# Transposing 18 of 32 blocks by DMA, as two 16-bit planes, in a transformer block on one Trainium2 core

## The chip, the core and the metric

The kernel runs on one core of a Trainium2 chip: TensorE (PE in the profile; PEld is its weight load), VectorE (DVE), ScalarE (ACT), GpSimd (POOL) and the queue engine SyncE (SP), each with its own in-order stream of instructions, and 16 DMA engines. The metric is the device time of one execution in microseconds, the median of three runs. The profile is one execution recorded by the hardware profiler.

## The reference

One pre-norm transformer block on 2048 rows of 512 floats, in float32.

```python
x = A_x                                          # (1, 2048, 512)
h = x + attention(layernorm(x), wqkv) @ wo       # 32 heads of 16; row s sees rows s, s-2, ..., s-14
n = layernorm(h)
r = relu(n @ w1 + b1)                            # 512 -> 1792
out = h + (r * r) @ w2 + b2                      # 1792 -> 512
```

Attention is local and dilated: each row has 8 keys (window 8, dilation 2), masked where the position is negative, softmax over the 8.

## The kernel before

**Numbers in two parts.** Every float32 matrix is split into a rounded part and the rest (`hi` on ACT, L141, and `lo` on DVE or POOL, L144); a product is three products of parts, so `mm3` (L224) is 12 matmuls of 128x128 by 128x512. A contraction needs the contracted dimension on the partitions, so three things are transposed on PE: the normalised input (`x_T`), attention's result (`o_T`) and the normalised residual (`h_T`). `transposes` (L199) is four 128x128 matmuls with the identity into one PSUM bank; `hi_T` and `lo_T` then read that bank and write the two parts. The second and fourth tile of the last group are transposed by the same four matmuls at L638.

**Tiles and stages.** The rows are 16 tiles `t` of 128, in 4 groups `u` of 4 tiles; t = 4u + i. Stage one computes q, k, v of tiles 0 to 3; stage two (`first_phase`, called for t0 = 4, 6, ..., 14) those of the other tiles, two a phase, in 12 half slots `m` a phase; a running number `k` = 12 (t0/2) - 72 + m gives the half slot relative to the phase of t0 = 12. Then come three loops over `u` = 0, 1, 2 with 17 slots `p` each: slot p holds a first-layer product `mlp1` (L224, from p = 0 to 13) and a second-layer product `mlp2` (L808, from p = 3 to 16) of group u. In the same slots group u + 1 goes through attention's tail: `load_h`, `o_T`, `wo_product` (L224, `wo<-`), the residual sum `h_add` (L577, DVE), `h_norm` (L194, ACT), `add_b2` (L587, POOL), a spill to memory, and `h_T`, whose parts are the input of the next loop. The last group (u = 3) has a stage of its own with seven products of halves (L731).

**Attention** runs on DVE and POOL beside all this: for each chunk `s` of two tiles (8 chunks) and each group of 4 heads (8), DVE multiplies (L335), sums (L369) and weighs (L346) blocks of 128x1024, POOL adds up the weighed blocks (L403, the last of three sums writes `o`), ACT copies q to PSUM (L264) and takes the exponentials (L392), and SP loads windows of k and v (L243) and q (L256) from memory, two steps ahead. A chunk is done after 8 sums into its `o`.

**The order** is written out by the program itself (a manual schedule): each engine executes in the order in which the Python code emits. `at(d, f, ...)` puts a call at the end of the slot d slots on, `after` behind it; `end_slot` runs the due calls, then `pump`. `pump` (L409 on) emits attention's steps as long as its own running estimate of DVE's time, `now["dve"]`, is below that of PE's, `now["pe"]`; an attention step counts as its cost times a factor from `SLOW`: the first for the stages before the loops, the second for loop u = 0, the third for the loops after. `transposes` adds 0.44 to PE's estimate. `pump(until=s)` emits attention until chunk s is done, whatever the estimates say; `o_T` calls it. `OT`, `WO`, `HT` are the half slots k of `o_T`, `wo_product`, `h_T` for tiles 0 to 3; `OP`, `WP`, `HP` the slots p for the four tiles of each later group (`HL` replaces `HP` in loop u = 2).

**Buffers.** Tiles named with `row(...)` share 15 buffers of 128x512 float32. In the loops the products and the transposes take turns on two PSUM banks (`mm0`, `mm1`).

Of the kernel before, what the change touches and what calls it, by code (L numbers as in the profile page):

```python
# [7 lines left out]

F32 = mybir.dt.float32
F32R = mybir.dt.float32r  # L10
AF = mybir.ActivationFunctionType
ALU = mybir.AluOpType
X = mybir.AxisListType.X
# [2 lines left out]
P = 128  # L16
KB = D // P
FB = F // P
R = 4
RI = 2  # L20
# [7 lines left out]
NEG = -4.0e9  # L28
ROWS = 15
LAG = 3  # L30
SLOW = 1.01, 1.12, 1.08
DELAY = 3
WJ = 2
XT = (9, 11), (7, 8)
OT = 4, 5, 10, 12
WO = 7, 9, 13, 15
HT = 20, 20, 21, 23
W2 = (18,)
LH = 3, 4, 10, 11
OP = 6, 7, 12, 13  # L40
WP = 8, 9, 13, 14
HP = 15, 15, 16, 16
UP = 14, 14, 15, 15
HL = (14, 0), (14, 1), (15, 0), (15, 1)
# [8 lines left out]
def block_kernel(ctx, tc, x, wqkv, wo, w1, b1, w2, b2, out):  # L53
    nc = tc.nc
# [3 lines left out]
    att = ctx.enter_context(tc.tile_pool(name="att", bufs=2))  # L58
# [27 lines left out]

    big_h = wpool.tile([P, 3 * KB, D], F32R, name="big_h")
    big_l = wpool.tile([P, 3 * KB, D], F32R, name="big_l")
    wq_h, wq_l = [t.rearrange("p (k c) n -> p k (c n)", k=KB) for t in (big_h, big_l)]
    wo_h = wpool.tile([P, KB, D], F32R, name="wo_h")  # L90
    wo_l = wpool.tile([P, KB, D], F32R, name="wo_l")
    w1_h = wpool.tile([P, KB, F], F32R, name="w1_h")
    w1_l = wpool.tile([P, KB, F], F32R, name="w1_l")
    w2_h, w2_l = {}, {}

    def row(name, shape=(P, D), dt=F32):
        return work.tile(list(shape), dt, name=name, tag="row", bufs=ROWS)
# [8 lines left out]
    def at(delta, fn, *a):  # L106
        due.setdefault(now["slot"] + delta, []).append((fn, a))
# [61 lines left out]
    def act_stats(key, src):  # L169
# [4 lines left out]
        scrap = row("scrap")  # L174
        nc.scalar.activation(scrap, src, AF.Identity, accum_out=nm[:, 0:1])
        nc.scalar.activation(nm[:, 1:2], nm[:, 0:1], AF.Identity, scale=-1.0 / D)
# [30 lines left out]
    def hi_T(tr, h_dst):  # L207
        for d, src in parts(tr, h_dst):
            hi(d, src)

    def lo_T(tr, h_dst, l_dst):
        for (d, src), h in zip(parts(tr, l_dst), h_dst):
            lo(nc.vector, d, src, h)
            dve(0.16 + 0.53 / len(h_dst))
# [16 lines left out]
    o_t = {}  # L231
# [177 lines left out]
    def pump(until=None):  # L409

        while (done[until] < G) if until is not None else (now["dve"] < now["pe"]):
            todo = sums[:]
            sums.clear()
            t = next(stream, "end")
            for a in todo:
                add_up(*a)
            if t == "end":
                now["dve"] = 1e9
                return
            if t is None:  # L420
                now["dve"] = max(now["dve"], now["pe"])
                return
            dve(t * SLOW[min(now['sub'] + 1, 2)])

# [126 lines left out]
    hs, hn = {}, {}  # L551
    oT = {}
# [9 lines left out]
    def o_T(t):  # L562
        s, j = divmod(t, RI)
        pump(until=s)
        tr = transposes(o_t[s][:, j, :])
        if t % R == RI:

            ohl = att.tile([P, 2, KB, P], F32R, name="ohl", tag="o", bufs=3)
            oT[t] = ohl[:, 0], ohl[:, 1]
        else:  # L570
            oT[t] = row("oh", (P, KB, P), F32R), row("ol", (P, KB, P), F32R)
        at(0, hi_T, tr, [oT[t][0]])
        at(0, lo_T, tr, [oT[t][0]], [oT[t][1]])

    def h_add(t, ps):
        h = hs[t]
        nc.vector.tensor_tensor(out=h, in0=ps, in1=h, op=ALU.add)  # L577
        dve(0.7)
        norm_stats(t, h)
# [16 lines left out]
    def wo_product(t, slots):  # L596
# [4 lines left out]
        for n, (fn, a) in zip(slots, ((h_add, (t, ps)), (h_norm, (t,)), (add_b2, (t,)),  # L601
# [5 lines left out]
    hh, hl = [[big_l[:, n:n + 2].rearrange("p k (i c) -> p k i c", i=R) for n in ns]  # L607
              for ns in ((0, 3), (6, 9))]

    def h_T(t):  # L610
        if t // R == R - 1:
            return last_h_T(t)
        tr = transposes(hn.pop(t), "mm")
        i = t % R
        hs_, ls_ = [a[:, :, i] for a in hh], [a[:, :, i] for a in hl]
        if len(turn["mm"].tags) > 2:
            at(0, hi_T, tr, hs_)
        else:
            due.setdefault(now["slot"], []).insert(0, (hi_T, (tr, hs_)))
        at(0, lo_T, tr, hs_, ls_)  # L620
# [7 lines left out]
    last_tr, banks = {}, {}  # L628
# [260 lines left out]
    for n in range(16):  # L889
        gp, t = divmod(n, 4)  # L890
# [27 lines left out]
    def first_phase(t0):  # L918
        def chores(m):
            if t0 + 3 < 16:  # L920
                if m in (0, 2):
                    at(0, x_stats, t0 + 2 + m // 2)

                early = t0 == 12
                if m + early in (6, 7):
                    at(0, x_norm, t0 - 4 + m + early)
                if m in XT[early]:
                    x_T(t0 + 2 + XT[early].index(m))
            if t0 + 5 < 16 and m in (6, 9):
                at(0, load_x, t0 + 2 + m // 3)  # L930
            if jobs and m % 3 == 0:
                at(0, weight_job)
            k = t0 // 2 * 12 - 72 + m
            if k == 19:
                dve(HOLD)
            for t in range(R):
                if k == OT[t]:
                    at(0, load_h, t)
                    o_T(t)
                if k == WO[t]:  # L940
                    wo_product(t, (1, 3, 4, 6))
                    now["pe"] += 2.73
                if k == HT[t]:
                    h_T(t)
            if k in W2:
                at(0, load_w2, W2.index(k))

        def half(m):
            end_slot(1.37)
            chores(m)  # L950

        for n in range(6):
            chores(2 * n)
            qkv_of(t0 + n % 2, n // 2, lambda: half(2 * n + 1))
            end_slot(1.37)
# [41 lines left out]
    for u in range(R - 1):  # L997
        now["sub"] = u
        first, end = u == 0, False
        fs = list(range(FB)) if first else [*sorted(place), 12, 13]  # L1000
        fs += [f for f in range(12) if f not in fs and (u < 2 or f not in ENDS)]
        fs += ENDS if u == 2 else []
        need = [] if first else [f for f in fs if f < 12 and f not in place]
        acc = [psum.tile([P, D], F32, name="acc", tag=tag) for tag in ("acc0", "acc1", "tr0", "tr1")]
        js = range(R)


        todo, halves = {}, {}
        for i in js:
            t = R * (u + 1) + i  # L1010
            if not end:
                a = i // 2 if u == 2 else 0
                for p, *what in ((LH[i] - a, at, 0, load_h, t), (OP[i] - a, o_T, t),
                                 (WP[i] - a, wo_product, t, (0, 1, 2 + 3 * a, 3 + 3 * a))):
                    todo.setdefault(p, []).append(what)
                p, h = (HP[i], i % 2) if u < 2 else HL[i]
                (todo, halves)[h].setdefault(p, []).append((h_T, t))
            todo.setdefault(UP[i], []).append((at, 0, unspill, R * u + i))
        if u == 2:
            for p, *what in ((12, at, 0, t_load, 0), (12, at, 0, t_load, 1), (13, after, 0, t_sums, 0),  # L1020
                             (13, after, 0, t_sums, 1), (13, at, 1, t_split, 0),
                             (14, after, 0, t_split, 1)):
                todo.setdefault(p, []).append(what)

        def half(p):
            run(due)
            for fn, *a in halves[p]:
                fn(*a)

        for p in range(FB + LAG):  # L1030
            more = 0.0
            if p == FB:
                run(due)
                dve(HOLD)
            if u < 2 and p == FB - 2:
                dve(HOLD)
            for fn, *a in sorted(todo.get(p, []), key=lambda x: x[0] is wo_product):
                fn(*a)
                more += 2.73 if fn is wo_product else 0.0
            if p < FB:  # L1040
                mlp1(u, fs[p])
                more += 2.73
                if first:
                    at(0, split_w2, p)
                    if p + 1 < FB:
                        load_w2(p + 1)
            q = p - LAG
            if q >= 0:
                f = fs[q]
                mlp2(u, f, acc, js, q == 0, q == FB - 1,  # L1050
                     (lambda: half(p)) if p in halves else None)
                more += 2.74
                if f < 12 and (need or first and p < FB - LAG):
                    free.append(place.pop(f))
                    if need:
                        at(1, fetch, need.pop(0))
            end_slot(more)
        for i in js:
            at(u // 2, finish, R * u + i, acc[i])
# [48 lines left out]
    h = hs[S // P - 1]  # L1108
# [34 lines left out]
```

## Time and profile before

| what | value |
|---|---|
| median of 3 runs | 514.47 us (514.29 to 515.16) |
| the profiled execution | span 513.0 us from the first to the last instruction; the page has no other time of it |
| PE, PEld busy | 506.4, 429.3 us |
| DVE, POOL, ACT busy | 376.7, 350.0, 256.2 us |
| matmuls that transpose | x 64, `o` 64, normalised residual 56 + 8 |
| moved by DMA | 97.37 MB, mean 190 GB/s |

A row of a grouped view reads: line, engine, operation, what is written and read, shapes, count, then busy time in us and the mean of one in ns, then the engine's idle time just before these instructions and what ended it. A row of the time line has the start in us from the span's beginning, the duration, and merged neighbours as x4. A row of the waits reads: who waited for whom, us in total, times, longest. Matmuls overlap in the records, so the step from one to the next is their price, not their duration.

### The profile page before, as it was taken

What the parts mean: (1) busy time and instruction counts of PE and PEld (TensorE: products, weight loads), DVE (VectorE), ACT (ScalarE), POOL (GpSimd) and SP (SyncE); (2) the same over time, 40 slices, a digit from 0 to 9 for tenths busy, and PEclk for the clock granted to TensorE, in tenths of its full rate; (3) what the DMA queues carried; (4) which work ended last, traced back from release to release, by engine and by line L of the source; (5) the groups of instructions that cost most, each with busy time, mean ns of one, the idle gap of its engine ahead of it and who ended that gap; (6) DMA issues with size and microseconds to landing.
All of it is one profiled execution on the core that took longest, in us unless ns stands there. A gap on an engine that the chain in (4) does not pass through costs nothing.

```text
span 513.0 us, 7625 instructions
## 1 busy us (share of the span) xinstructions
PE 506.4 (99%) x2508; PEld 429.3 (84%) x2508; DVE 376.7 (73%) x524; ACT 256.2 (50%) x498; POOL 350.0 (68%) x430
## 2 busy tenths in 40 slices
PE   7999999999999999999999999999999999999997
PEld 6999788888888888888888888888888888989996
DVE  5489799988998798976889799778984035742333
ACT  4634687767424763463364334336432525666542
POOL 4714888894885895896778759676889544685520
PEclk9999999999999999999999999999999999999999
DMA  9677989889677895685487537557632352454112
GB/s 265 193 221 188 271 283 315 275 274 278 196 234 201 291 299 173 175 232 180 129 266 229 163 94 231 174 160 257 219 94 65 106 159 84 142 145 145 63 41 82
DMA packets 88239, 97.37 MB, mean 190 GB/s; under 512 B 8328, under 2 KB 56712, under 8 KB 88200
## 3 DMA queue, kind: packets, MB, share of 16 engines
q1 hardware_dynamic: 87256, 96.37, 61.4%
q10 hardware_dynamic: 944, 0.52, 0.3%
q8 instruction: 19, 0.31, 0.3%
q14 instruction: 20, 0.16, 0.1%
HBM read 72.65 MB, written 24.25 MB: 189 GB/s over the span
## 4 chain that ended last, share of the span: by engine, by line
PE 92%; POOL 3%; DMA 2%; DVE 1%; issue 1%; ACT 1%; SPq 0%; POOLq 0%; ACTq 0%
PE mm L224 45%; PE acc L808 29%; PE wo L224 9%; PE mm L731 6%; PE tr L199 4%; DMA wraw<-in_A_wqkv_dram 1%; DMA qkv_d<-y 1%; POOL pr L403 1%; POOL h L587 1%; POOL tl L144 0%; PE half L831 0%; SPq L432 0%; POOL wo_l L144 0%; DVE pr L346 0%; DVE ex L369 0%
## 5 line engine op out<-in xcount | busy, mean ns | idle before, releaser
L403 POOL TENSOR_TENSOR pr<-pr 128x512 f32<-128x512 f32 (+1 forms) x128 | 132.1, 1032 | 51.2 <-DVE pr L346 45.7
L224 PE MATMUL mm<-big_l,w_h 128*128 128x512 f32 x336 | 89.5, 392 | 0.0
L346 DVE TENSOR_TENSOR pr<-ex,v 128x1024 f32<-128x1024 f32 x64 | 78.0, 1221 | 11.6 <-POOL o L403 7.6
L335 DVE TENSOR_TENSOR pr<-qp,k 128x1024 f32<-128x1024 f32 x64 | 76.8, 1201 | 5.7 <-ACT qp L264 5.7
L369 DVE TENSOR_REDUCE ex<-pr 128x64 f32<-128x1024 f32 x64 | 78.4, 1225 | 1.8
L224 PEld LDWEIGHTS mm<-big_l,w_h 128*128 128x128 f32 x336 | 62.3, 188 | 12.8 <-DVE ol L144 0.2
L144 POOL TENSOR_TENSOR rl<-r,rh 128x512 fp32r<-128x512 f32 x42 | 55.4, 1318 | 22.5 <-ACT rh L141 22.4
L224 PE MATMUL mm<-big_h,xl 128*128 128x512 f32 (+1 forms) x208 | 55.9, 379 | 0.2 <-DVE xl L144 0.2
L224 PE MATMUL mm<-big_h,xh 128*128 128x512 f32 (+1 forms) x208 | 53.5, 378 | 0.7 <-ACT xh L141 0.7
L784 ACT ACTIVATE r<-mm,b_sb 128x512 f32<-128x512 f32 x42 | 28.8, 686 | 47.9 <-PE mm L224 46.1
L224 PE MATMUL mm<-big_l,xh 128*128 128x512 f32 (+1 forms) x208 | 52.7, 375 | 0.0
L808 PE MATMUL acc<-big_l,rh 128*128 128x512 f32 x190 | 52.7, 391 | 0.0
L808 PE MATMUL acc<-big_h,rh 128*128 128x512 f32 x190 | 52.3, 392 | 0.0
L808 PE MATMUL acc<-big_h,rl 128*128 128x512 f32 x190 | 51.8, 390 | 0.0
L493 ACT COPY y<-mm 128x512 f32<-128x512 f32 (+1 forms) x52 | 28.6, 552 | 40.0 <-PE mm L224 30.1
L224 PE MATMUL mm<-big_l,w_l 128*128 128x512 f32 x168 | 45.0, 390 | 0.0
L224 PEld LDWEIGHTS mm<-big_h,xh 128*128 128x128 f32 x208 | 37.6, 188 | 7.0 <-ACT xh L141 1.7
L224 PEld LDWEIGHTS mm<-big_l,xh 128*128 128x128 f32 x208 | 38.2, 188 | 6.0
L224 PEld LDWEIGHTS mm<-big_h,xl 128*128 128x128 f32 x208 | 37.2, 188 | 5.7 <-DVE xl L144 0.6
L808 PEld LDWEIGHTS acc<-big_h,rl 128*128 128x128 f32 x190 | 35.7, 188 | 7.5
L808 PEld LDWEIGHTS acc<-big_l,rh 128*128 128x128 f32 x190 | 35.4, 188 | 7.3
L808 PEld LDWEIGHTS acc<-big_h,rh 128*128 128x128 f32 x190 | 34.8, 188 | 6.5
(148 smaller groups left out, 879.8 us busy)
## 6 DMA issues: line engine op xcount, KB each, us to landing
k<-qkv_d SPq DMA_DIRECT2D x48, 288.0 KB, 2.8
v<-qkv_d SPq DMA_DIRECT2D x48, 288.0 KB, 4.0
qkv_d<-y SPq DMA_DIRECT2D x18, 512.0 KB, 4.3
big_l<-w2l_d SPq DMA_DIRECT2D x24, 256.0 KB, 3.1
xt<-in_A_x_dram SPq DMA_DIRECT2D x16, 256.0 KB, 4.3
q<-qkv_d SPq DMA_DIRECT2D x32, 128.0 KB, 3.0
h<-in_A_x_dram SPq DMA_DIRECT2D x16, 256.0 KB, 4.1
h_d<-h SPq DMA_DIRECT2D x16, 256.0 KB, 4.1
```

What stands on the lines that cost most here:

```text
L144: eng.tensor_tensor(out=dst, in0=src, in1=h, op=ALU.subtract)
L199: nc.tensor.transpose(tr[:, k, :], src[:, k * P:(k + 1) * P], ident)
L224: nc.tensor.matmul(ps, l(k), r(k), start=(n == 0), stop=(n == 3 * KB - 1))
L335: nc.vector.tensor_tensor(out=pr.rearrange("p i w h d -> p i w (h d)"), in0=qps["now"][:, j % 2].unsqueeze(2).to_broadcast([P, RI, W, GC]) ...
L346: nc.vector.tensor_tensor(out=p2, in1=vwin, op=ALU.mult, in0=e1[:, :, :, j * GH:(j + 1) * GH].unsqueeze(4).to_broadcast([P, RI, W, GH, DH]))
L369: nc.vector.tensor_reduce(out=lf[:, :, :, j * GH:(j + 1) * GH], in_=pr, axis=X, op=ALU.add)
L403: nc.gpsimd.tensor_tensor(out=dst, in0=p2[:, :, :w], in1=p2[:, :, w:2 * w], op=ALU.add)
L493: nc.scalar.copy(y[:, :, t % RI * GC:(t % RI + 1) * GC], ps[:, :j * GC].rearrange("p (j c) -> p j c", j=j))
L587: nc.gpsimd.tensor_tensor(out=h, in0=h, in1=b2_sb, op=ALU.add)
L731: nc.tensor.matmul(ps, sta[y][:, k], mov[x][:, k], start=(first and q == 0), stop=(last and q == len(terms) - 1), skip_group_check=True)
L784: nc.scalar.activation(r, ps, AF.Relu, bias=b1_sb[:, f:f + 1])
L808: nc.tensor.matmul(acc[j], l[:, j * P:(j + 1) * P], w[f], start=(first and n < len(js)), stop=(last and n >= len(terms) - len(js)))
```

## The change

For tiles in `OV` (10 of attention's 16) and `HV` (8 of the 16 normalised residuals) the transposition leaves PE. A float32 block of 128x512 is copied by ACT into two planes of 16-bit halves (split), SP issues one transposing DMA of the 128x1024 16-bit elements back into the source's buffer, eight blocks of 128x128, and ACT puts the halves together again (join); `hi_T` and `lo_T` then read this SBUF tile instead of a PSUM bank. Split, DMA and join stand in three slots: for tiles 0 to 3 by `OK` and `HK`, in the loops from `OP` on (o0, o0 + 1, o0 + 2), and from `WP` + 2 on for the residual. In the loops the `wo` products of each group's first two tiles move one slot later (`WP`). The second and third pacing factor are lowered.

```diff
-SLOW = 1.01, 1.12, 1.08
+OV = (0, 1, 2, 3, 4, 5, 8, 9, 12, 13)
+HV = (0, 1, 4, 5, 8, 9, 12, 13)
+SLOW = 1.01, 1.10, 1.06
+OK = (-6, -2, 4), (-5, -1, 5), (3, 6, 10), (4, 7, 12)
+HK = (12, 15, 18), (14, 16, 19)
-WP = 8, 9, 13, 14
+WP = 9, 10, 13, 14
+    def turn_split(key, src):
+        planes[key] = src, row("pl")
+        nc.scalar.copy(two_planes(planes[key][1]), halves_of(src))
+
+    def turn_dma(key):
+        src, pl = planes[key]
+        nc.sync.dma_start_transpose(
+            src.bitcast(U16).rearrange("p (n c) -> p n c", c=P), pl.bitcast(U16))
+
+    def turn_join(key):
+        src, pl = planes[key]
+        nc.scalar.copy(halves_of(pl).rearrange("p two n -> p n two"),
+                       two_planes(src).rearrange("p two n -> p n two"))
+        planes[key] = pl.rearrange("p (k c) -> p k c", k=KB)
+
+    def o_split(t):
+        s, j = divmod(t, RI)
+        pump(until=s)
+        turn_split(("o", t), o_t[s][:, j, :])
+
+    def o_join(t):
+        turn_join(("o", t))
+        tr = planes.pop(("o", t))
...
+        hi_T(tr, [oT[t][0]])
+        lo_T(tr, [oT[t][0]], [oT[t][1]])
+
+    def h_split(t):
+        turn_split(("h", t), hn.pop(t))
+
+    def h_parts(t):
+        i = t % R
+        tr = planes.pop(("h", t))
+        if t // R == R - 1:
+            last_tr[i] = tr
+            split_last(i, tr)
+            return
...
+        hi_T(tr, hs_)
+        lo_T(tr, hs_, ls_)
                 if k == OT[t]:
                     at(0, load_h, t)
-                    o_T(t)
+                    if t not in OV:
+                        o_T(t)
+                if t in OV and k in OK[t]:
+                    at(0, (o_split, lambda t: turn_dma(("o", t)), o_join)[OK[t].index(k)], t)
+                if t in HV and k in HK[t]:
+                    at(0, (h_split, lambda t: turn_dma(("h", t)),
+                           lambda t: turn_join(("h", t)))[HK[t].index(k)], t)
...
-                    h_T(t)
+                    (at(0, h_parts, t) if t in HV else h_T(t))
...
-                for p, *what in ((LH[i] - a, at, 0, load_h, t), (OP[i] - a, o_T, t),
+                o0 = OP[i] - a
+                if t in OV:
+                    turned = [(o0, at, 0, o_split, t), (o0 + 1, at, 0, turn_dma, ("o", t)),
+                              (o0 + 2, at, 0, o_join, t)]
+                else:
+                    turned = [(o0, o_T, t)]
+                if t in HV:
+                    h0 = WP[i] - a + 2
+                    turned += [(h0, at, 0, h_split, t), (h0 + 1, at, 0, turn_dma, ("h", t)),
+                               (h0 + 2, at, 0, turn_join, ("h", t))]
...
-                (todo, halves)[h].setdefault(p, []).append((h_T, t))
+                if t in HV:
+                    todo.setdefault(p, []).append((at, 0, h_parts, t))
+                else:
+                    (todo, halves)[h].setdefault(p, []).append((h_T, t))
```

More of the change, by code (lines that the diff above doesn't have):

```diff
@@ L10 @@
 F32R = mybir.dt.float32r
+U16 = mybir.dt.uint16
 AF = mybir.ActivationFunctionType
@@ L573, in o_T, with halves_of, two_planes @@
         at(0, lo_T, tr, [oT[t][0]], [oT[t][1]])
+    planes = {}
+    def halves_of(a):
+        return a.bitcast(U16).rearrange("p (n two) -> p two n", two=2)
+    def two_planes(a):
+        return a.bitcast(U16).rearrange("p (two n) -> p two n", two=2)
+    def turn_split(key, src):
[17 more added lines that the diff above has]
+        tr = planes.pop(("o", t))
+        if t % R == RI:
+            ohl = att.tile([P, 2, KB, P], F32R, name="ohl", tag="o", bufs=3)
+            oT[t] = ohl[:, 0], ohl[:, 1]
+        else:
+            oT[t] = row("oh", (P, KB, P), F32R), row("ol", (P, KB, P), F32R)
+        hi_T(tr, [oT[t][0]])
[9 more added lines that the diff above has]
+            return
+        hs_, ls_ = [a[:, :, i] for a in hh], [a[:, :, i] for a in hl]
+        hi_T(tr, hs_)
+        lo_T(tr, hs_, ls_)
     def h_add(t, ps):
@@ L1012, in block_kernel @@
                 a = i // 2 if u == 2 else 0
-                for p, *what in ((LH[i] - a, at, 0, load_h, t), (OP[i] - a, o_T, t),
+                o0 = OP[i] - a
[8 more added lines that the diff above has]
+                               (h0 + 2, at, 0, turn_join, ("h", t))]
+                for p, *what in ((LH[i] - a, at, 0, load_h, t), *turned,
                                  (WP[i] - a, wo_product, t, (0, 1, 2 + 3 * a, 3 + 3 * a))):
@@ L1016, in block_kernel @@
                 p, h = (HP[i], i % 2) if u < 2 else HL[i]
-                (todo, halves)[h].setdefault(p, []).append((h_T, t))
+                if t in HV:
+                    todo.setdefault(p, []).append((at, 0, h_parts, t))
+                else:
+                    (todo, halves)[h].setdefault(p, []).append((h_T, t))
             todo.setdefault(UP[i], []).append((at, 0, unspill, R * u + i))
```

## The prediction, as it was made before the result

> **What bounds the kernel now.** First the busy times and the chain that ended last, both on the page of the profile.
>
> ```profile
> span 513.0 us, 7625 instructions
> PE 506.4 (99%) x2508; PEld 429.3 (84%) x2508; DVE 376.7 (73%) x524; ACT 256.2 (50%) x498; POOL 350.0 (68%) x430
> ...
> PEclk9999999999999999999999999999999999999999
> ...
> PE 92%; POOL 3%; DMA 2%; DVE 1%; issue 1%; ACT 1%; SPq 0%; POOLq 0%; ACTq 0%
> ```
>
> TensorE (PE) is busy 506.4 of 513.0 us at a granted clock in the top digit in all 40 slices, and 92% of the last chain is its own work. So PE time that goes away is time saved, as long as nothing makes PE wait instead. Next I read the windows, one row a stage, for the engines that could (us, then busy time of PE, PEld, DVE, ACT, POOL, then clock, DMA share, GB/s).
>
> ```profile
> 120.00:162.00 42.00, 42.00 (x206) 34.91 (x205) 37.34 (x53) 18.93 (x40) 27.08 (x38) 1.00 0.76 230
> 162.00:210.00 48.00, 48.00 (x217) 39.70 (x216) 41.45 (x50) 27.17 (x48) 37.01 (x39) 1.00 0.75 237
> 210.00:254.00 44.00, 43.98 (x206) 35.94 (x205) 35.24 (x49) 19.32 (x38) 36.64 (x42) 1.00 0.66 194
> 254.00:300.00 46.00, 46.00 (x208) 38.10 (x207) 40.59 (x49) 20.63 (x36) 30.40 (x33) 1.00 0.62 190
> 300.00:345.00 45.00, 45.00 (x212) 37.26 (x211) 37.06 (x50) 17.70 (x34) 36.15 (x46) 1.00 0.59 181
> 345.00:390.00 45.00, 45.00 (x204) 37.24 (x203) 39.13 (x47) 20.02 (x34) 35.38 (x39) 1.00 0.57 181
> ```
>
> While attention runs, PE never idles. VectorE (DVE) is busy 37.34 + 41.45 + 35.24 + 40.59 + 37.06 + 39.13 = 230.8 of 270 us, so 39 us are free; ScalarE (ACT) is under 60% and the DMA engines under 76%. DVE is the engine nearest to PE. The view of waits says why part of its idle time is there, and how little PE waits for what the change touches (total, times, longest):
>
> ```profile
> DVE h L577 <- PE wo L224: 16.9, 11, 6.5
> ...
> PEld tr L199 <- ACT hn L194: 0.4, 1, 0.4
> ...
> PEld mm L224 <- DVE ol L144: 0.2, 1, 0.2
> ```
>
> DVE stands 16.9 us waiting for PE's `wo` product: it runs ahead of PE, and those waits shrink by themselves if PE comes earlier.
>
> **The change, part by part. Removed from PE:** 18 blocks of four transposes. The price of a block is read from the time line as the distance between the same matmuls with and without one between them.
>
> ```profile
> 218.19 1.07 PE L808 MATMUL acc<-big_h,rh 128*128 128x512 f32 x4
> ...
> 223.63 1.07 PE L808 MATMUL acc<-big_h,rh 128*128 128x512 f32 x4
> ...
> 226.35 0.60 PE L199 MATMUL tr<-ident,o 128*128 128x128 f32 x4
> ...
> 229.54 1.07 PE L808 MATMUL acc<-big_h,rh 128*128 128x512 f32 x4
> ```
>
> Without a block 223.63 - 218.19 = 5.44 us pass, with one 229.54 - 223.63 = 5.91, so a block holds PE 0.47 us. 18 x 0.47 = 8.46 us go. This is the only term on the path, and the greatest gain there can be.
>
> **Added to ACT:** two copies a block (split and join), 36 in all, each of 1024 16-bit elements. Rows of the grouped view, busy us, then mean ns:
>
> ```profile
> L141 ACT CAST rh<-r 128x512 fp32r<-128x512 f32 x56 | 34.8, 622 | 2.2
> ...
> L144 DVE TENSOR_TENSOR rl<-r,rh 128x512 fp32r<-128x512 f32 x14 | 11.8, 842 | 22.5 <-ACT rh L141 21.2 <-POOL traw L701 1.3
> ...
> L144 DVE TENSOR_TENSOR ol<-tr,oh 128x512 fp32r<-128x512 f32 x12 | 8.3, 690 | 10.3 <-ACT oh L141 10.1 <-POOL w_l L144 0.2
> ...
> L141 ACT CAST th<-traw 128x1024 fp32r<-128x1024 f32 x7 | 7.3, 1050 | 4.9 <-POOL traw L702 4.9
> ...
> L141 ACT CAST oh<-tr 128x512 fp32r<-128x512 f32 x12 | 7.0, 586 | 8.5 <-PE tr L199 8.5
> ```
>
> No row has 16-bit elements. The ends are 0.62 us (a 512-element row, if two halves go as one word) and 2.1 (twice the 1024-element row, if 16-bit strides cost double); I take 1.05, the row with as many elements. That is 37.8 us: 12.6 around the first phases' window of 120 to 162, where ACT has 42 - 18.9 = 23 free, and 25.2 over the three loops, where about half of it is free. PE hides it; at 2.1 us the first phases would lack 2 us. The casts and subtractions now read SBUF instead of PSUM: 622 against 586 ns on ACT, up to 842 against 690 on DVE, together at most 18 x 0.15 = 2.7 us of DVE's 39 idle: nothing on the path.
>
> **Added to SP and the DMA queue:** 18 transfers of 256 KB. The trace has no transposing one. The page's issue lines (KB each, median us to landing) and the queue's line give the nearest:
>
> ```profile
> q1 hardware_dynamic: 87256, 96.37, 61.4%
> ...
> out_dram<-h SPq DMA_DIRECT2D x15, 256.0 KB, 2.7
> ...
> raw<-in_B_w_dram SPq DMA_DIRECT2D x14, 256.0 KB, 5.8
> ...
> b_sb<-in_B_b_dram SPq DMA_DIRECT2D x1, 7.0 KB, 4.6
> ```
>
> Plain transfers of this size land in 2.7 to 5.8 us: the near end. The far end is the bias load: 1,792 pieces of 4 bytes in 4.6 us. If every 2-byte element were a piece of its own, 131,072 of them would take 73 times that, 336 us. If a run of 128 neighbours is a piece, there are 1,024, fewer than the bias load has. I take 5 us, the rows that it is nearest to. On the engines a packet costs 0.614 x 513 x 16 / 87256 = 58 ns on average, so 1,024 of them hold all 16 for 3.7 us and 18 transfers for 67 us at most, which the idle quarter and more takes.
>
> The Trainium skill (page "VectorE: DVE Perf Modes", section "The three transpose paths") speaks against the change: 1309 ns for one 128x128 16-bit block through the DMA, and its rules prefer TensorE where a PSUM result will do. By it, as an estimate, eight blocks one after another land after 10.5 us, and the sum would be that of the first rival. Another page of the Trainium skill ("DMA: Bandwidth & Descriptors", section "Latency and other measured facts") gives 261 GB/s for DMA transposes, an estimate of 1.0 us for 256 KB, by which my sum stands. No run here shows either.
>
> **The added wait.** The join waits on ACT for the landing. Behind it stand ACT's casts, attention's `qp` copies and exps, then the eviction of the next hidden block; behind the cast, DVE's subtraction and every attention step after it. How late may it land? For tile 4 (group 0):
>
> ```profile
> 193.22 0.60 PE L199 MATMUL tr<-ident,o 128*128 128x128 f32 x4
> ...
> 207.31 1.07 PE L224 MATMUL wo<-wo_h,oh 128*128 128x512 f32 x4
> ```
>
> ```profile
> 194.94 0.32 SPq L989 DMA_DIRECT2D w2l_d<-big_l  x1
> ```
>
> ```profile
> 202.07 0.69 DVE L577 TENSOR_TENSOR h<-wo,h 128x512 f32<-128x512 f32 x1 [1.71 <-PE wo L224]
> ```
>
> Slot 7 begins at 193.22; SP reaches the work of its end (the stash, L989) at 194.94, so the transposing transfer goes out near 195.3. Tile 4's `wo` product moves from slot 8 to slot 9, which began at 207.31; without slot 8's product (2.72 us) and one block it begins at 204.1. Join 1.05 and cast 0.62 come before it: a landing time up to 204.1 - 195.3 - 1.67 = 7.1 us costs PE nothing. DVE arrives at slot 8's end near 200.4 (202.07 less its wait of 1.71) and so far waits there for PE until 202.07; with 5 us it waits for the cast until 195.3 + 5 + 1.67 = 202.0, the same. Above 5 us DVE loses what is over, per block of `o`.
>
> **What is late next** is attention itself. Tiles 6, 10 and 14 are still transposed by PE, and PE comes to them earlier. Their last sums on POOL, counted back from the last of the 64 (8 per chunk: the 33rd, 17th and 1st from the end), and PE's transposes of 10 and 14:
>
> ```profile
> 223.02 0.47 POOL L403 TENSOR_TENSOR o<-pr 128x128 f32<-128x128 f32 x1
> ...
> 315.41 0.47 POOL L403 TENSOR_TENSOR o<-pr 128x128 f32<-128x128 f32 x1
> ...
> 394.33 0.47 POOL L403 TENSOR_TENSOR o<-pr 128x128 f32<-128x128 f32 x1
> ```
>
> ```profile
> 317.52 0.60 PE L199 MATMUL tr<-ident,o 128*128 128x128 f32 x4
> ...
> 402.94 0.60 PE L199 MATMUL tr<-ident,o 128*128 128x128 f32 x4
> ```
>
> By tile 6, 8 blocks are gone (3.76 us): PE comes at 222.6, the sum ends at 223.5, 0.9 late. By tile 10, 12 blocks (5.64): PE at 311.9, sum at 315.9, 4.0 late. By tile 14, 16 blocks (7.52): 395.4 against 394.8, in time. If attention keeps its clock, PE therefore waits 4.0 us in all; if DVE gains what its waits for PE give back, 0. The lower factors serve this: the walk credits PE 0.44 us a block, 7.0 us less over 16 blocks, and 1.12 to 1.10 and 1.08 to 1.06 place 1.8 to 1.9% more attention per slot, some 3 us of DVE's 193 us in the loops (the last five windows), most of which is attention. I take the middle, 2.0 us of new waiting.
>
> **Sum:** 513.0 - 8.46 + 2.0 = 506.5 us of span. The profile gives no time beside its span; the median of the runs, 514.47, is 1.47 above it, so 508.0 us. Own range 506.0 (no wait) to 510.0 (4.0).
>
> **Rivals.** *Late landing* (the one that ends slower): at the six `o` blocks of the loops PE waits for the join at `wo`, each us above 7.1 once per block. Six of them eat the gain from 7.1 + 8.46 / 6 = 8.5 us on; at twice the longest row, 11.6 us, it is 506.0 + 6 x 4.5 = 533, or 519.5 if in each pair the first wait covers the second. For it: nothing here shows such a transfer. Against: the plain rows. Chance 0.15.
>
> *Attention starved*: between 5 and 7 us, or with `k` and `v` loads queued behind the transfers, DVE loses about 1 us at each of the four blocks before tile 10, and PE waits there 4.0 + 4 = 8 us: 514; with half a us at each, 512, which I take for its middle, and I let it spread from 510 to 516. For it: a DVE that is 85% busy in these windows. Against: its 39 us idle. Chance 0.25 (0.16 faster, 0.06 same, 0.03 slower).
>
> *Buffers*: the 15 row buffers now hold the planes too, and a load on SP waits until one is free. The queue's waits have one such today:
>
> ```profile
> SPq L594 <- PE acc L808: 7.0, 1, 7.0
> ```
>
> One more of the kind that PE feels by 3 of the 7 us gives 511; against it, a plane is held while the two parts of `o` aren't yet. Chance 0.05. That PE keeps its transposes I exclude: the calls are gone.
>
> **Numbers.** Forecast 0.55, rivals 0.15, 0.25, 0.05. Faster by over 0.2% (about what a measurement of this kernel can tell from no change) 0.55 + 0.16 + 0.05 = 0.76, within 0.06, slower 0.15 + 0.03 = 0.18. The range reaches from 505.3 (no wait, less the runs' scatter) to 514.5, and leaves out the late landing and the top of the second rival, about 0.2.
>
> **What would show it.** Right: transposes of `o` 24 and of `hn` 32 on PE, PE busy near 498 us, the transposing transfers landing in 4 to 7 us, ACT near 290 us busy, a wait of PE (or PEld) for POOL's `o` at L199 of 0 to 4 us at tiles 6 and 10. Wrong: PE waiting at `wo` for `oh`, or DVE's busy share falling between 162 and 320 us with waits for ACT's casts or for `k` and `v`.

## The result: 2.1% slower, and the profile after

The changed kernel takes 525.92 us (median of 4 runs, 525.46 to 526.17) against 514.38 (4 runs, 514.11 to 515.16) for the kernel before on the same chip: ratio 1.0214, 95% interval 1.0201 to 1.0227. The forecast was 508.0 us, with a range up to 514.5. The profiled execution has a span of 524.0 us, 11.0 more than before. In the profile after, lines behind the insertions have other numbers: L144 (`lo`) is L149, L141 (`hi`) L146, L199 (transposes) L204, L224 (`mm3`) L229, L403 (`o`) L408; L591 is the split, L595 the transposing DMA, L600 the join.

First the page of the kernel after:

```profile
span 524.0 us, 7551 instructions
...
PE 504.3 (96%) x2436; PEld 426.1 (81%) x2436; DVE 382.9 (73%) x524; ACT 293.5 (56%) x534; POOL 351.4 (67%) x430
```

72 transposing matmuls (18 blocks of four) are gone, as intended. But PE is busy 504.3 us, only 2.1 less than before where 8.46 less were due, and idle 524.0 - 504.3 = 19.7 us instead of 513.0 - 506.4 = 6.6. So, at the predicted price of a block, the span's change has three parts: -8.46 of removed work, +13.1 of idle time, and +6.4 of work that is the same but takes longer: -8.46 + 13.1 + 6.4 = 11.0. The view of waits says whom PE waited for, before and then after (who for whom, us in total, times, longest):

```profile
PE tr L856 <- POOL mhalf L842: 1.3, 1, 1.3
PE tr L199 <- DVE xt L190: 1.1, 1, 1.1
```

```profile
PE tr L204 <- POOL o L408: 8.4, 2, 4.5
PE tr L204 <- ACT xt L199: 3.1, 2, 2.5
```

Two new waits for POOL's `o`, 8.4 us, are attention coming late; one wait of 2.5 us for ACT's `xt` is new too. None is for a join or for `oh` at `wo`. Windows of 5 us at the three (PE busy is the first number behind the length; the granted clock stands third from the end) give the slower work:

```profile
125.00:130.00 5.00, 2.51 (x11) 2.07 (x11) 2.53 (x4) 4.91 (x9) 1.14 (x1) 0.86 1.09 374
130.00:135.00 5.00, 5.00 (x21) 4.00 (x21) 4.90 (x7) 2.54 (x6) 0.41 (x1) 0.80 1.03 219
...
235.00:240.00 5.00, 5.00 (x18) 4.01 (x18) 4.02 (x5) 1.82 (x4) 3.78 (x4) 0.72 0.81 230
...
330.00:335.00 5.00, 5.00 (x16) 4.01 (x17) 3.77 (x6) 0.94 (x2) 2.52 (x3) 0.67 0.51 106
```

After each of these three waits the clock falls to 0.67 to 0.80 for some 5 us. That is 1.0 + 1.4 + 1.65 us in the windows that begin at 130, 235 and 330 and 0.35 in the one at 125, 4.4 of the 6.4.

What the added operations cost, from the issue lines (median us to landing) and the groups of the kernel after:

```profile
o<-pl SPq DMA_TRANSPOSE x10, 4.0
hn<-pl SPq DMA_TRANSPOSE x8, 4.5
```

```profile
L600 ACT COPY pl<-o 128x1024 uint16<-128x1024 uint16 x10 | 11.7, 1169 | 2.5 <-DMA o<-pl 2.5
...
L591 ACT COPY pl<-o 128x1024 uint16<-128x1024 uint16 x10 | 10.4, 1040 | 1.6 <-POOL o L408 1.6
...
L149 DVE TENSOR_TENSOR ol<-pl,oh 128x512 fp32r<-128x512 f32 x9 | 9.0, 1002 | 12.7 <-ACT oh L146 12.7
```

The transfers land in 4.0 to 4.5 us and the joins wait 2.5 us for those of `o` in all and 0.3 for those of `hn`. Not the DMA, then; the question is why attention is late.

How late it is can be read from POOL's time line, where before had the 33rd sum from the end (the one that tile 6 needs) at 223.02 us and the 17th (tile 10) at 315.41. After:

```profile
234.21 0.46 POOL L408 TENSOR_TENSOR o<-pr 128x128 f32<-128x128 f32 x1
...
329.46 0.46 POOL L408 TENSOR_TENSOR o<-pr 128x128 f32<-128x128 f32 x1
```

They start 11.2 and 14.05 us later than before, the last sum 16.1. The lag is 0.8 us at the 14th of the 64 sums (108 us) and 9.7 at the 18th (147): most of it arises in the first phases, where tiles 0 to 3 have six turned blocks (four of `o`, two of the residual).

### The profile page after: what moved, and what is told of

The parts are those of the page before. It is cut to its first block, busy times and chain, and to the rows that moved or that the text cites. A ratio compares the mean times of both kernels' runs of the same rounds, so it can differ in the third digit from the quotient of the medians.

```text
span 524.0 us, 7551 instructions
## 1 busy us (share of the span) xinstructions
PE 504.3 (96%) x2436; PEld 426.1 (81%) x2436; DVE 382.9 (73%) x524; ACT 293.5 (56%) x534; POOL 351.4 (67%) x430
## 3 DMA queue, kind: packets, MB, share of 16 engines
q1 hardware_dynamic: 106264, 101.09, 64.4%
## 5 line engine op out<-in xcount | busy, mean ns | idle before, releaser
L408 POOL TENSOR_TENSOR pr<-pr 128x512 f32<-128x512 f32 (+1 forms) x128 | 133.3, 1042 | 56.7 <-DVE pr L351 50.9
L229 PE MATMUL mm<-big_l,w_h 128*128 128x512 f32 x336 | 90.8, 397 | 1.4 <-ACT y L498 1.0
L229 PEld LDWEIGHTS mm<-big_l,w_h 128*128 128x128 f32 x336 | 64.0, 192 | 15.4 <-ACT y L498 1.4
L149 POOL TENSOR_TENSOR rl<-r,rh 128x512 fp32r<-128x512 f32 x42 | 54.9, 1309 | 20.1 <-ACT rh L146 18.3
L229 PE MATMUL mm<-big_h,xl 128*128 128x512 f32 (+1 forms) x208 | 55.7, 379 | 0.2 <-DVE xl L149 0.2
L229 PE MATMUL mm<-big_h,xh 128*128 128x512 f32 (+1 forms) x208 | 53.1, 377 | 0.7 <-ACT xh L146 0.7
L229 PE MATMUL mm<-big_l,xh 128*128 128x512 f32 (+1 forms) x208 | 52.8, 375 | 0.0
L229 PE MATMUL mm<-big_l,w_l 128*128 128x512 f32 x168 | 46.1, 398 | 0.0
L229 PEld LDWEIGHTS mm<-big_h,xh 128*128 128x128 f32 x208 | 37.9, 188 | 7.2 <-ACT xh L146 1.5
L229 PEld LDWEIGHTS mm<-big_l,xh 128*128 128x128 f32 x208 | 38.2, 188 | 6.0
L229 PEld LDWEIGHTS mm<-big_h,xl 128*128 128x128 f32 x208 | 37.3, 188 | 5.8 <-DVE xl L149 0.6
```

What stands on the lines that cost most here:

```text
L149: eng.tensor_tensor(out=dst, in0=src, in1=h, op=ALU.subtract)
L229: nc.tensor.matmul(ps, l(k), r(k), start=(n == 0), stop=(n == 3 * KB - 1))
L408: nc.gpsimd.tensor_tensor(out=dst, in0=p2[:, :, :w], in1=p2[:, :, w:2 * w], op=ALU.add)
```

## Experiments

Kernels measured together share their runs of before (medians 514.84, 515.01, 514.96 and 514.34 us in the four groups), so the ratios are compared.

| kernel | us | ratio, 95% interval |
|---|---|---|
| the change | 525.92 | 1.0214 (1.0201 to 1.0227) |
| e1 loops' 12 blocks | 512.83 | 0.9960 (0.9945 to 0.9975) |
| e2 as e1, factors of before | 517.55 | 1.0067 (1.0042 to 1.0093) |
| e3 tiles 0 to 3's 6 blocks | 529.30 | 1.0287 (1.0267 to 1.0307) |
| e4 the change, factors of before | 535.07 | 1.0390 (1.0370 to 1.0410) |
| e5 ACT's copies alone | 516.03 | 1.0027 (1.0017 to 1.0037) |
| e6 the DMAs alone | 515.40 | 1.0007 (0.9997 to 1.0017) |
| e7 as e3, slots moved | 531.82 | 1.0330 (1.0314 to 1.0345) |
| e8 the change, slots moved | 525.80 | 1.0208 (1.0184 to 1.0233) |
| e9 as e3, credit put back | 520.03 | 1.0109 (1.0084 to 1.0134) |
| e10 before, credit taken away | 526.52 | 1.0220 (1.0201 to 1.0238) |
| e11 as e9, subtraction later | 518.53 | 1.0064 (1.0051 to 1.0077) |
| e12 the change, both | 515.39 | 0.9998 (0.9983 to 1.0012) |
| e13 as e12, tiles 0 and 1 on PE | 511.99 | 0.9951 (0.9938 to 0.9964) |
| e14 the change, credit put back | 518.78 | 1.0084 (1.0071 to 1.0097) |
| e15 as e13, lower factors | 513.13 | 0.9973 (0.9961 to 0.9986) |

**Where does it arise?** Theory A: in the six blocks of tiles 0 to 3, by what they add to ACT and DVE in the first phases. Rival B: the transposing transfers and SP's issuing of them. The halves, and the two loads by themselves:

```diff
 e1
-OV = (0, 1, 2, 3, 4, 5, 8, 9, 12, 13)
-HV = (0, 1, 4, 5, 8, 9, 12, 13)
+OV = (4, 5, 8, 9, 12, 13)
+HV = (4, 5, 8, 9, 12, 13)
 e3 (WP and SLOW as before)
+OV = (0, 1, 2, 3)
+HV = (0, 1)
 e5: before, with 12 ACT copies of a constant block in the slots of those splits and joins
+    nc.scalar.copy(...)      # 128x1024 16-bit elements, results unused
 e6: before, with 18 transposing DMAs of a constant block in the slots of the change
+    nc.sync.dma_start_transpose(...)      # results unused
```

> Only the twelve blocks of the three loops are transposed by DMA; tiles 0 to 3 (four blocks of o, two of the residual) stay on TensorE; pacing factors and the later wo slots as in the changed kernel. Theory A (the copies on ScalarE in the first phases put attention some 11 us behind, and PE pays for that at tiles 6 and 10 and in a lower clock after each wait): attention is on time again at 162 us, 12 x 0.47 = 5.6 us are gained, at most 1.5 us given back at tile 10: 509 to 511 us. Rival B (the transfers themselves, through SP's time and the loads of k and v behind them, or the joins in the loops): twelve of eighteen are still there, 518 us or more. Rival C (the lower factors): 518 us or more as well, since they stay.

> Only the six blocks of tiles 0 to 3 are transposed by DMA; the loops, the wo slots and the pacing factors are those of the kernel before. Theory A: attention some 10 us late at 162 us as in the changed kernel, PE waits for the input's normalisation near 125 us and for attention in the loops: 518 to 525 us although 6 x 0.47 = 2.8 us of PE are gone. Rival B (transfers): a third of them, 512 to 516. Rival C (factors): 512 us.

> The kernel before, all transposes on TensorE, with twelve added copies of 128x1024 16-bit elements on ScalarE, in the half slots where the changed kernel splits and joins tiles 0 to 3; they read a constant and nobody reads what they write. It computes the same result. Theory A (ScalarE's time alone does it): 12.6 us more on ScalarE, xt and the casts late near 110 to 131 us, attention 6 to 10 us behind: 517 to 523 us. If the chain split, transfer, join, cast, subtract is needed for the delay, not ScalarE's load: 514 to 516. Rivals B and C: 514.4 us.

> The kernel before, all transposes on TensorE, with eighteen added transposing DMAs of the same size in the same slots, from a constant into a spare row buffer; nobody reads what they write. Theory A: 514.4 us, within 1. Rival B (SP's time and the DMA engines): 518 us or more. Rival C: 514.4.

The loops' blocks alone are 0.4% faster than before, the six alone 2.9% slower: the place is shown. The transfers alone cost nothing that can be told (0.07%, interval over 1), so B falls. But ACT's copies alone cost only 0.27% (e1 and e3 also missed their expected figures, by 2 and 4 us): ACT's load isn't the cause either, and A explains too little.

**Is it the slots?** Theory A2: the places of split, DMA and join in the order of the engines' work.

```diff
 e7 (on e3), e8 (on the change)
-OK = (-6, -2, 4), (-5, -1, 5), (3, 6, 10), (4, 7, 12)
+OK = (-4, -1, 5), (-3, 0, 7), (8, 9, 12), (9, 10, 14)
 e2 (on e1), e4 (on the change)
-SLOW = 1.01, 1.10, 1.06
+SLOW = 1.01, 1.12, 1.08
```

> Only the six blocks of tiles 0 to 3, as in the run of the first phases alone (529.3 us), with the same instructions, but the splits and joins of the four blocks of o in other half slots: splits at -4, -3, 8, 9 instead of -6, -5, 3, 4, transfers at -1, 0, 9, 10, joins at 5, 7, 12, 14. They then stand behind the normalisation of x on ScalarE and no longer reach the head of its queue before POOL has written o. Theory A2 (the order on ScalarE: a split that waits for POOL's o with the normalisation of x, the evictions and the casts behind it): TensorE's wait for xt and the clock's fall after it go, attention is at most 4 us late at 162 us, 511 to 515 us. Rival (ScalarE's time and the longer chain to DVE's subtraction, wherever they stand): 519 us or more.

> The changed kernel with the same four pairs of half slots moved. Theory A2: the gain of the loops (512.8 us alone) and up to 2.8 us for tiles 0 to 3, 509 to 513 us. Rival: 519 us or more.

> The twelve blocks of the loops alone (512.8 us) with the pacing factors of before, 1.12 and 1.08. If the lower factors are what keeps attention up: PE waits for attention's sums at tiles 6 and 10 again, 2 to 4 us more, 514.5 to 517. If they do harm: 510 to 512. If neither: 512.8 within 0.8.

> The changed kernel with the pacing factors of before and nothing else. Attention is 11 us late at 162 us either way. If the lower factors help it to catch up: 528 to 533 us, longer waits at tiles 6 and 10. If they are a cause of the loss (rival C): below 520 us.

Moving the slots changed nothing in the time (1.0208 against 1.0214) or made it worse: A2 falls. It did move a wait: in e8 PE waits no more for ACT's `xt`, but twice 2.0 us at `wo` for ACT's casts. The factors matter: the old ones cost 1.1% in e2 and 1.8% in e4 (0.5 and 2 us above the top of what was expected). So what counts is how far ahead the program places attention, and that pointed to theory D.

**The lost credit.** `transposes` adds 0.44 us to `now["pe"]`; a turned block doesn't. For the six blocks of the first phases that is 2.64 us by which `pump` thinks PE is earlier, and the factor there stayed 1.01. Counted along DVE's instructions, before has 108 attention steps ahead of tile 6's subtraction and 156 ahead of tile 10's; e3 has 106 and 154, the change 107 and 154, e9 again 108 and 156. Rival E: DVE's own waits in the first phases, for the chain of split, DMA, join and cast, and for a full ACT.

```diff
 e9 (on e3), e14 (on the change)
     def o_join(t):
         turn_join(("o", t))
+        if t < R:
+            now["pe"] += 0.44
...
     def h_parts(t):
         i = t % R
+        if t < R:
+            now["pe"] += 0.44
 e10: before, nothing turned
         tr = transposes(o_t[s][:, j, :])
+        if t < R:
+            now["pe"] -= 0.44
...
         tr = transposes(hn.pop(t), "mm")
         i = t % R
+        if t < 2:
+            now["pe"] -= 0.44
```

> Only the six blocks of tiles 0 to 3 are turned by DMA, with the factors and wo slots of before (as in the run that gave 529.3 us), and PE's estimate is credited 0.44 us for each of these blocks where its transposes stood, though PE no longer does them. By the kernels' text, attention's DVE steps then stand exactly where before had them (108 ahead of tile 6's lower part, 156 ahead of tile 10's; without the credit 106 and 154). Theory D (the lost credit puts attention two steps later on DVE, PE waits for it at tiles 6, 10 and 14 and loses clock): 513 to 517 us, PE's waits for POOL's o under 2 us. Rival E (the longer chain from split to subtraction makes DVE lose some 5 us in the first phases, and that is what PE waits for later): 524 us or more, waits as without the credit.

> The kernel before, every transpose still on PE, no split, join or transposing DMA; only PE's estimate loses the 0.44 us for the six blocks of tiles 0 to 3. Attention's DVE steps then stand where the run with these six blocks alone had them (106 ahead of tile 6's lower part, 154 ahead of tile 10's, against 108 and 156). Before has 2.9 us to spare at tile 6 and 1.6 at tile 10. Theory D: two steps are 2.5 us, so PE waits 0 to 1 us at tile 6, 1 to 2 at tile 10, and loses some clock: 515.5 to 519 us. Rival E: 514.3 to 515.4, no change.

> The change itself with one thing more: PE's estimate is credited 0.44 us for each of the six blocks of tiles 0 to 3. Theory D: most of the loss goes, 516 to 519 us, and PE waits under 2 us for POOL's o (8.4 in the change); the rest, against the 515.4 with the subtraction a slot later, is what the chain on ACT and DVE costs. If the credit mattered only because the factors were those of before: 523 us or more.

e10 has the very instructions of before and only another order: 2.2% slower, far above the 515.5 to 519 that I expected, and as slow as the change. D is shown. The busy line and the wait for `o` of its profiled run, on the page and in the view of waits:

```profile
span 525.9 us, 7614 instructions
...
PE 511.3 (97%) x2508; PEld 432.5 (82%) x2508; DVE 375.3 (71%) x524; ACT 256.7 (49%) x498; POOL 349.5 (66%) x430
```

```profile
PE tr L199 <- POOL o L403: 5.8, 2, 3.4
```

The six blocks alone (e3) have the same wait, 5.8 us in two times, the longest 3.5. In e10 2508 matmuls as before take 511.3 instead of 506.4 us, 4.9 more, and idle time is 8.0 us more. Why two steps of 1.2 us cost so much is seen at tile 6, on PE's, DVE's and POOL's time line of e10:

```profile
227.35 0.49 PE L199 MATMUL tr<-ident,o 128*128 128x128 f32 x3
231.28 0.33 PE L199 MATMUL tr<-ident,o 128*128 128x128 f32 x1 [3.44 <-POOL o L403]
231.36 1.89 PE L224 MATMUL mm<-big_l,w_h 128*128 128x512 f32 x4
```

```profile
221.85 1.22 DVE L346 TENSOR_TENSOR pr<-ex,v 128x1024 f32<-128x1024 f32 x1
...
227.51 1.26 DVE L144 TENSOR_TENSOR big_l<-raw,big_h 128x512 fp32r<-128x512 f32 x1
232.26 0.69 DVE L144 TENSOR_TENSOR ohl<-tr,ohl 128x512 fp32r<-128x512 f32 x1 [3.49 <-ACT ohl L141]
232.87 1.21 DVE L335 TENSOR_TENSOR pr<-qp,k 128x1024 f32<-128x1024 f32 x1
```

```profile
224.44 1.30 POOL L144 TENSOR_TENSOR big_l<-raw,big_h 128x512 fp32r<-128x512 f32 x1
225.70 1.29 POOL L589 TENSOR_TENSOR h<-h,b_sb 128x512 f32<-128x512 f32 x1
226.95 1.27 POOL L144 TENSOR_TENSOR rl<-r,rh 128x512 fp32r<-128x512 f32 x1
228.18 2.51 POOL L403 TENSOR_TENSOR pr<-pr 128x512 f32<-128x512 f32 x2
230.77 0.45 POOL L403 TENSOR_TENSOR o<-pr 128x128 f32<-128x128 f32 x1
```

PE stands for the last sum of `o`, which comes late. DVE had the product for it ready at 223.07, but POOL takes it up only at 228.18: with two steps fewer placed, the sum has slid behind three other operations in POOL's order (1.30 + 1.29 + 1.27 us). In before these three begin at 223.45, 224.70 and 226.48, behind the sum of 223.02; in e14 the sum (227.17) again stands ahead of such operations (from 228.93 on). DVE stands as well, 3.49 us, because the next thing in its order is the subtraction that follows PE's transposes; no attention is placed ahead of it, so the time isn't used and the lag grows. And after the wait four matmuls take 1.89 instead of 1.07 us. The same happens again at tile 10, where two operations of POOL stand ahead of the sum. The windows in which the clock is low hold some 2.6 of the 4.9 us of slower work; the rest isn't explained (e5 and e6, at a granted clock of 1.00 and with before's matmuls, show 508.0 and 507.6 us, so 1.2 to 1.6 us are found without any change in PE's work).

In the change itself the credit is worth 1.0214 - 1.0084 = 1.3%, 6.7 us, and PE's waits for POOL's `o` are gone from the view of e14:

```profile
PE tr L204 <- ACT xt L199: 2.9, 1, 2.9
PE mm L229 <- ACT r L847: 2.0, 2, 1.2
```

The rest isn't the credit. e9 came out at 520.0, above its 513 to 517, though PE waits no more for `o` in it: E has a share of its own.

**The chain and the queue on ACT.** On DVE's time line of the change, the two subtractions of tiles 0 and 1 wait for ACT's cast:

```profile
125.18 0.69 DVE L149 TENSOR_TENSOR ol<-pl,oh 128x512 fp32r<-128x512 f32 x1 [3.05 <-ACT oh L146]
...
129.30 0.69 DVE L149 TENSOR_TENSOR ol<-pl,oh 128x512 fp32r<-128x512 f32 x1 [2.29 <-ACT oh L146]
```

ACT's time line beside it has no gap, and a norm of `x` that PE waits for stands behind a split, a join and a cast:

```profile
121.55 1.03 ACT L591 COPY pl<-o 128x1024 uint16<-128x1024 uint16 x1
...
123.28 1.16 ACT L600 COPY pl<-o 128x1024 uint16<-128x1024 uint16 x1
124.47 0.62 ACT L146 CAST oh<-pl 128x512 fp32r<-128x512 f32 x1
125.00 1.04 ACT L591 COPY pl<-o 128x1024 uint16<-128x1024 uint16 x1
...
126.69 0.81 ACT L199 ACTIVATE xt<-xt,rs 128x512 f32<-128x512 f32 x1
```

```profile
124.45 0.61 PE L229 MATMUL mm<-big_h,xl 128*128 128x512 f32 x2
127.56 0.66 PE L204 MATMUL tr<-ident,xt 128*128 128x128 f32 x4 [2.49 <-ACT xt L199]
...
129.33 1.91 PE L229 MATMUL wo<-wo_h,ol 128*128 128x512 f32 x4
```

Three kernels take these apart: DVE's subtraction one slot later, and tiles 0 and 1 left on PE.

```diff
 e11 (on e9), e12 (on e14); the same for the residual's
-        lo_T(tr, [oT[t][0]], [oT[t][1]])
+        if t < R:
+            at(1, lo_T, tr, [oT[t][0]], [oT[t][1]])
+        else:
+            lo_T(tr, [oT[t][0]], [oT[t][1]])
 e13 (on e12)
-OV = (0, 1, 2, 3, 4, 5, 8, 9, 12, 13)
+OV = (2, 3, 4, 5, 8, 9, 12, 13)
 e15 (on e13)
-SLOW = 1.01, 1.10, 1.06
+SLOW = 1.01, 1.08, 1.04
```

> As the run with the credit put back for the six blocks, and DVE's subtraction of these blocks comes one slot later, so that DVE does attention while ACT joins and casts. Theory D alone: within 1 us of the run with the credit. If DVE's waits for ACT's casts in the first phases count as well (E beside D): 1 to 4 us faster than that run, down to 512 (before less 6 x 0.47 us), and DVE's waits for oh between 107 and 165 us under 3 us instead of 7 to 10.

> The whole change (18 blocks, its factors and slots), with the credit put back and the subtraction one slot later for the six blocks of tiles 0 to 3. By the text attention stands as in the run with the loops' blocks alone (108, 156). Theory D with E: that run's 512.8 less 6 x 0.47, 509 to 513 us, faster than before. If the six blocks cost for another reason: 518 us or more.

> The whole change with credit and later subtraction as in the run that gave 515.4 us, but tiles 0 and 1 keep o's transposes on PE (16 blocks turned instead of 18). Their splits, joins and casts fall on 107 to 131 us, where ACT was busy without a gap in the change and PE waited 2.6 us for ACT's xt at 122. If that queue on ACT is what is left of the loss: PE has no wait there, clock 1.00 from 107 to 165, and 512.8 less 4 x 0.47, 510 to 512 us. If the remaining loss lies with tiles 2 and 3 or with hn: 513.5 us or more.

> As the first kernel of this call, with the second and third factor at 1.08 and 1.04 instead of 1.10 and 1.06. By the text attention then stands 1 step further ahead at tile 6 and 2 at tile 10. If attention still sets the time in the loops: 0.5 to 1.5 us faster than the first kernel. If it is in time already (PE waits for joins and casts instead): the same within 0.5 us, or up to 2 us slower as residual sums and norms are queued behind attention on DVE.

The later subtraction takes 0.45% off e9 and 0.86%, 4.4 us, off e14; e12 is level with before, short of its 509 to 513. Leaving tiles 0 and 1 on PE takes off another 0.47%, 2.4 us, though PE has 0.94 us more to do. e13 is the best kernel of the study, 0.49% faster than before (0.36 to 0.62). Its page and waits:

```profile
PE 500.0 (98%) x2444; PEld 423.3 (83%) x2444; DVE 381.3 (75%) x524; ACT 288.8 (57%) x530; POOL 352.2 (69%) x430
```

```profile
PE tr L925 <- POOL mhalf L911: 1.3, 1, 1.3
PE mm L229 <- ACT r L853: 1.2, 1, 1.2
```

Lower factors on top (e15) gave 513.13 against 511.99: no gain, perhaps a loss. Attention is in time by then.

## Why the prediction was wrong, point by point

- **PE's price of a block, 0.47 us: not refuted, but not known better than to 0.1.** At a granted clock of 1.00 PE is busy (506.4 - 502.0) / 12 = 0.37 us a block less in e1 and (506.4 - 500.0) / 16 = 0.40 in e13. But against e5 and e6, which have before's matmuls and show 508.0 and 507.6, the same two give 0.47 to 0.50. At 0.39, 7.0 us went instead of 8.46, and the slower work in the change is 4.9 us instead of 6.4; the windows hold 4.4.
- **The failed step: "I take the middle, 2.0 us of new waiting".** It was bounded by 0 and 4.0 under "If attention keeps its clock". Attention didn't. The prediction named the credit ("0.44 us a block, 7.0 us less over 16 blocks") and set the lower factors against it. But the first factor stayed at 1.01 where the first six blocks lose theirs, and attention's DVE steps moved behind instructions that wait for PE (one of them at tile 6 and two at tile 10 in the change). It also took the time of POOL's sums as given, though their places in POOL's order come from the same walk. In the first phases DVE lost time to the chain as well: between 120 and 162 us it is busy 37.3 us in before, 34.2 in e10 and 31.8 in the change. Tiles 6 and 10 were the right places; 0.9 and 4.0 us of lateness at them, 4.0 us of waiting in all, became 8.4 us of waiting (4.5 and 3.9). With the waits for ACT, PE's idle time rose by 13.1 us where the sum had 2.0.
- **A term that was missing: the clock.** PE time was priced at the full clock throughout; 4.4 us of slower work lie in the windows behind the waits, and 4.9 to 6.4 there are in all.
- **"12.6 around the first phases' window of 120 to 162, where ACT has 42 - 18.9 = 23 free": wrong.** A copy costs 1.04 and 1.17 us, near the 1.05 taken, and ACT is busy 293.5 us, near the 290. But the joins of tiles 0 and 1 and the splits of tiles 2 and 3 meet at 121 to 129 us, where ACT then had no gap, and the average over 42 us hid that. With the credit, the later subtraction and without these two blocks the loss goes (e14, e12, e13).
- **DVE's subtraction from SBUF:** 1002 ns on average instead of 690 from PSUM, outside the "up to 842"; 0.31 us x 9 is 2.8 us for `ol`. But the mean mixes two kinds: five of the nine take 0.69 us, as from PSUM, and four 1.08 to 1.78. Those four each begin with 0.5 us or more left of an instruction of POOL, the other five with at most 0.14:

```profile
206.37 1.29 POOL L149 TENSOR_TENSOR rl<-r,rh 128x512 fp32r<-128x512 f32 x1
206.69 1.52 DVE L149 TENSOR_TENSOR ol<-pl,oh 128x512 fp32r<-128x512 f32 x1 [2.62 <-ACT oh L146]
```

  No run tried the subtraction by itself.
- **The landing of 5 us: right,** 4.0 and 4.5. On the page after, queue q1 has 106264 packets instead of 87256, 1056 more a transfer, near the 1,024 of "if a run of 128 neighbours is a piece". By the Trainium skill's page "VectorE: DVE Perf Modes", section "The three transpose paths", I had estimated 10.5 us; no trace here agrees with one 128x128 block after another at 1309 ns. The other estimate, 1.0 us from the 261 GB/s of "DMA: Bandwidth & Descriptors", section "Latency and other measured facts" in the Trainium skill, is the time of the bytes alone; issue to landing is four times that.
- **The 1.47 us from span to time: somewhat low.** It compares the span of one run with the median of others; the change's profiled run took 525.85 us with its span of 524.0, 1.85 more.
- **The rivals.** Late landing and buffers didn't happen. "Attention starved" had the right victim and the wrong cause (late landings or queued loads of `k` and `v`; e6 excludes both as a cost by themselves), and at 510 to 516 us was too small by 10, since it too left out the clock and the growing lag. The signs named for being wrong hardly showed: PE doesn't wait at `wo`, and DVE is busy 134.3 instead of 135.4 us between 162 and 320 us (its waits for ACT's `oh` there rose from 2.8 to 7.8). Most of the lag arose before that window, where no sign was set.

What stays open: the loops' 12 blocks alone gain 2.0 us where 5.6 were due (e1). By the page of e1, PE's busy time fell by 4.4 us and its idle time rose by 1.8; waits for ACT's `r` and `hn` are new:

```profile
PE 502.0 (98%) x2460; PEld 425.4 (83%) x2460; DVE 381.8 (75%) x524; ACT 281.0 (55%) x522; POOL 351.0 (69%) x430
```

```profile
PE mm L229 <- ACT r L843: 1.2, 1, 1.2
PE tr L204 <- ACT hn L199: 0.7, 1, 0.7
```

That is a span 2.6 us shorter. The median gains 0.6 us less because the profiled run, 512.18 us, is the fastest of e1's four; why idle time rose wasn't settled.

## What to carry to other kernels

Where a program places work by an estimate of its own, an instruction that is taken away also takes its entry out of the estimate: look which work moves behind which wait, and undo the entry alone as an experiment (e10 took no instruction away and lost as much as the change). Read an engine's free time in windows as short as the burst that is added, some 10 us here, not over a stage. And price a wait of PE of 2 us or more with the slower clock that may come behind it, 1.4 to 1.65 us each in the change.

## What was not expected of the hardware

- **The granted clock can fall after one wait.** After waits of 2.5 and 4.5 us in the change and 3.4 in e10 groups of four matmuls took up to 1.91 us instead of 1.07, and the window that follows showed 0.80, 0.72 and 0.66; the waits of up to 1.3 us in before left it at 1.00. The third is e10's:

```profile
230.00:235.00 5.00, 3.72 (x10) 2.95 (x11) 2.65 (x4) 1.10 (x2) 3.62 (x4) 0.66 0.43 162
```

  The length of the wait alone doesn't decide: one of 1.97 us in e8 brought the clock down, while one of 3.45 in e3 (and others of 2.62 in e2 and 2.79 in e4) left it at 1.00. What decides is not shown here. First e3's wait and the window behind it, then e8's:

```profile
234.28 0.33 PE L204 MATMUL tr<-ident,o 128*128 128x128 f32 x1 [3.45 <-POOL o L408]
```

```profile
235.00:240.00 5.00, 5.00 (x24) 4.07 (x23) 4.61 (x6) 2.69 (x5) 2.91 (x3) 1.00 0.34 84
```

```profile
140.54 2.87 PE L229 MATMUL wo<-wo_h,ohl 128*128 128x512 f32 x8 [1.97 <-ACT ohl L146]
```

```profile
140.00:145.00 5.00, 4.46 (x13) 3.36 (x14) 4.45 (x4) 2.08 (x4) 4.84 (x6) 0.69 1.17 266
```

  The Trainium skill (page "TensorE: Matmul & The Clock Gate", section "What's actually happening") tells of half the clock after an idle window of about 3.4 us and the full one again after a busy window as long, an estimate of 1.7 us lost each time. The trace agrees in the size, 1.65 us from the 0.67 over 5 us, but not in the length: 1.97 us were enough in e8 and 3.45 were not in e3.
- **SP is held by a transposing issue,** 1.25 to 1.46 us in these rows and 1.24 to 1.79 over the kernel, against 0.4 to 0.6 for the plain ones around it:

```profile
115.27 1.46 SPq L595 DMA_TRANSPOSE o<-pl  x1
116.83 0.51 SPq L248 DMA_DIRECT2D k<-qkv_d  x1
...
117.95 1.25 SPq L595 DMA_TRANSPOSE o<-pl  x1
```

  It cost nothing here (e6).
